# An attention block whose order of work is planned in Python: reciprocals of 16 columns, a broadcast in four transfers, and an order drawn from a table of seeds

## The chip, the core and the metric

The kernel runs on one core of a Trainium2 chip. Five engines matter here: TensorE (PE), VectorE (DVE), ScalarE (ACT), GpSimd (POOL) and SyncE (SP), which issues most of the transfers. Each engine takes its instructions in the order of the program and waits, at the head of its queue, for what the next one needs. The metric is the device time in microseconds (us) of the core. Three runs of the kernel before gave 408.4, 409.14 and 409.2; their median is 409.14 us.

## What is computed

The input is one sequence of 2048 tokens with 448 channels, 16 heads of 28 channels, everything in bf16:

```python
qkv = (x @ wqkv).reshape(B, S, 3, H, Dh)      # S = 2048, D = 448, H = 16, Dh = 28
scores = einsum("bhqd,bhkd->bhqk", q, k) * Dh ** -0.5
p = softmax(scores, axis=-1)
o = einsum("bhqk,bhkd->bhqd", p, v)
out = o.reshape(B, S, D) @ wo
```

Nothing is masked, so 16 x 2048 x 2048 scores need an exponential each.

## The kernel before, in words

**Tiles.** The heads are worked in four groups of four, the queries in four chunks of 512. A group and a chunk make a window; there are 16. In a window the keys come in 16 rows of 128, and a row has four tiles, one for each head: a tile is 128 keys by 512 queries. All in all there are 16 x 16 x 4 = 1024 tiles, each one score matmul (L917); two of them run side by side on two halves of PE's rows.

**Two ways to an exponential.** Pairs of tiles go into a two-bank PSUM tile `PA` (two of them), and ACT turns a pair into bf16 probabilities `PTA` in one instruction (L1337). The other tiles go singly into one of three banks `PD` and are turned into the bits of an exponential by a polynomial: `DU` (DVE, L1118), `DV` (DVE, L1121), `DG` (POOL, L1124) and `PTD` (DVE, L1137), or, for a few, one DVE copy to `SG` (L1050) and six POOL steps (L1057 to L1080). In the profile, 844 tiles go to ACT as 422 pairs, 155 go the way of DVE with one POOL step, and 25 the way of POOL.

**After the exponential.** PE multiplies the probabilities with the values `VA` and adds them up in the bank `PO` (L1182). One column in eight of `VA` is 1.0, so that some rows of `PO` hold the softmax's sums. When a window is through, `finish_window` runs a chain: DVE copies `PO` to `OSB` (L1002); SP sends the rows with the sums to `DCO`, spread over 128 partitions (L1009); DVE takes the reciprocals, `DRC` (L1011); SP sends them to a DRAM scratch `SCR` (L1012) and back, broadcast over the partitions, to `RRB` (L1014); POOL multiplies `OSB` by `RRB` into `OT` (L1017). The last window takes the reciprocals with DVE's block transposes instead (`norm_dve`, L929 to L933), and the output follows by matmuls with `WO` (L856, L876, L951, L1469).

**What sets the order.** No order is written out by hand. The kernel holds a list of operations (`Op`), each with an engine, a planned duration, a latency until others can use its result, what it depends on, and a priority. A loop at the end of the kernel plays them through in planned time: whenever an engine is free in the plan, it takes the ready operation with the lowest priority number (`try_static` for DVE, POOL and SP; `try_pe` and `try_act` for the other two). PE decides there whether the next tile goes to a free `PA` pair or to a free `PD` bank, that is, to ACT or to DVE, so the number of tiles on each way falls out of the planned times. What was planned is then written out, engine by engine, and the chip runs it in that order with real waits; planned times themselves are not in the program. Constants such as `P1`, `PTT`, `XLAT0`, `GLAT` and the numbers inside `Op(...)` are planned durations and latencies.

**The start.** SP loads one half of the first chunk of `x` and then `WQ`; ACT's queue loads `WK` and then the other half (L281, L286). PE transposes the chunk in two rounds of eight (L418) into four banks, ACT and DVE copy two of the four pieces each (L425), PE forms the first queries and keys (L534), ACT writes `QB` twice (L709, L711) and `KB` twice (L571), DVE reduces the keys to a bound (L562), and the exponentials begin.

Of the kernel before, what the change touches and what calls it, by code (L numbers as in the profile page):

```python
# [9 lines left out]
ACT = mybir.ActivationFunctionType  # L10
# [4 lines left out]
F32 = mybir.dt.float32  # L15
# [34 lines left out]
PTT = 1.12  # L50
PTS = 0.59
# [33 lines left out]
def kernel(  # L85
# [38 lines left out]
    GEND = 0  # L124
    GY = 0.5
# [17 lines left out]
    GLAT = 2.4  # L143
# [46 lines left out]
    XLAT0 = (4.0, 4.8)  # L190
# [49 lines left out]
    DCW = QW * NR // P  # L240
# [5 lines left out]
    SCR = [dram.tile([NR, QW], F32, name=f"SCR{i}") for i in range(2)]  # L246
# [164 lines left out]
    t0_bank = (PO[:], PA[1][:, 0:QW], PA[0][:, 0:QW], PA[0][:, QW:2 * QW])  # L411
# [9 lines left out]
    for cc in range(CC):  # L421
        eng = ("ACT", "DVE")[cc % 2]

        def ev0(cc=cc, eng=eng):
            (nc.scalar.copy if eng == "ACT" else nc.vector.tensor_copy)(  # L425
                out=XT[0][cc // 2][:, cc % 2, :], in_=t0_bank[cc].bitcast(BF16)[0:CK, 0:QW])
        xt0.append(add(Op(eng, 0.48 if eng == "ACT" else 0.36, ev0, deps=[t0[0][cc], t0[1][cc]], prio=-4999 + cc)))
# [53 lines left out]
    wkin = add(Op("SP", 0.01, None, prio=-1999, lat=5.1))  # L481
    wqin = add(Op("SP", 0.01, None, prio=-1998, lat=WQLAT))
    wvin = add(Op("SP", 0.01, None, prio=-1997, lat=11.0))
    for (W, WP, nm, win) in ((WK, WKP, "k", wkin), (WQ, WQP, "q", wqin)):
        w_ready[(nm, 0)] = add(Op("POOL", 1.0, pad_w(W, WP, 0), deps=[win], prio=-5001 + (nm == "k")))
# [181 lines left out]
    def task_Q(g, c):  # L667
# [38 lines left out]
        if w < NF:  # L706
            pq = -4390 if w == 0 else Q1P - 900
            if w == 0:
# [3 lines left out]
                    out=qb[1][:], in_=ap(), func=ACT.Identity, bias=offscol[:, 0:1], scale=YSC), deps=[ops[-1]], prio=pq + 15, lat=0.17))  # L712
# [17 lines left out]
            for i in range(HG):  # L730
                o = bound(i, [ab, kmaxop[0][0]] + ([e1] if w or i > 1 else []), pq + (20 if i < 2 else 40) + 0.01 * i)
# [261 lines left out]
    def finish_window(w, pvop):  # L993
# [11 lines left out]
        def rel(t):  # L1005
# [4 lines left out]
            out=DCO[b][:], in_=OSB[b][RS - 1::RS, :].rearrange("i (a b) -> i a b", b=DCW)), deps=[ev], prio=-10, lat=2.6))]  # L1010
        o2 = add(Op("DVE", 0.22, lambda: nc.vector.reciprocal(out=DRC[b][:], in_=DCO[b][:]), deps=o1, prio=-4000))  # L1011
        o3 = add(Op("SP", 0.4, lambda: nc.sync.dma_start(out=SCR[b][:].rearrange("i (a b) -> (i a) b", b=DCW),  # L1012
                                                         in_=DRC[b][:]), deps=[o2], prio=-10, lat=2.0))
        o4 = [add(Op("SP", 0.6, lambda: nc.sync.dma_start(  # L1014
            out=RRB[b][:], in_=bass.AP(SCR[b][:].tensor, SCR[b][:].offset, [[QW, NR], [0, RS], [1, QW]])),
            deps=[o3], prio=-10, lat=GLAT))]
# [205 lines left out]
    def try_pe(t):  # L1222
# [35 lines left out]
        if acts and not starved and (not TW or kmax_op[0].end is not None) and fits(MM, "S") and pos[0] < NT - NTAIL and s_ready(pos[0], t) and d_inflight[0] < ND + (OD > 0):  # L1258
# [4 lines left out]
            if free:  # L1263
# [37 lines left out]

    act_log = []
# [16 lines left out]
    def try_act(t):  # L1319
# [4 lines left out]
        if act_i[0] < len(acts):  # L1324
# [14 lines left out]
            op = Op("ACT", 0.0633 + 0.4267 * len(ns), fn, kind="E", lat=ELAT)  # L1339
# [18 lines left out]
    def try_static(e, t):  # L1358
        best = None
        for o in static[e]:  # L1360
            if o.elig is not None and not o.elig(t):
                continue
            if best is not None and o.prio >= best.prio:
                continue
            if o.kind == "sb" and (lock[0] > t + 1e-9 or YIELD and pool_waits(t)):
                continue
            if all(d.done(t) for d in o.deps) and (o.acq is None or o.acq(t)):
                best = o
# [13 lines left out]
    while True:  # L1382
# [12 lines left out]
        while progress:  # L1395
            progress = False
            for e in ("ACT", "PE", "POOL", "DVE", "SP"):
# [32 lines left out]
                seq += 1  # L1430
                heapq.heappush(ends, (o.end, seq, o))
# [74 lines left out]
```

## Time and profile before

One execution was profiled. Its own time was 408.98 us, 0.16 us under the median of the three runs; the span of its records is 407.2 us, so 1.8 us lie around the records.

| | busy, us | share of the span | instructions |
|---|---|---|---|
| PE | 358.5 | 88% | 2611 |
| DVE | 379.2 | 93% | 659 |
| ACT | 395.3 | 97% | 434 |
| POOL | 341.9 | 84% | 369 |

How to read it: a group's row gives line, engine, operation, output<-input, the count, the busy time of the group (overlaps counted once), the mean duration of one in ns, and the engine's idle time just before these instructions with what ended it. A record of ACT or DVE is longer than the distance to the next, because the next one begins before the last result is written. The clock of PE was granted in full in every slice of the span. The transfers move 17.16 MB, 42 GB/s on average.

### The profile page before, as it was taken

To read this page: it belongs to the slowest core of one execution; us is meant where nothing else is said; L and a number is where in the kernel's file an instruction comes from. 1 tells how busy PE (TensorE), PEld (TensorE's weight loads), DVE (VectorE), ACT (ScalarE), POOL (GpSimd) and SP (SyncE) were. 2 spreads that over 40 slices of the span, in tenths; PEclk is the share of its full clock that TensorE was granted. 3 is DMA by queue.
4 is the path that set the end of the run, shared out by engine and by line. 5 is a ranking of instruction groups with operands and counts; after the bars stand their busy time and mean duration, and the time that the engine had idled before them with its cause. 6 is when DMAs were issued, how large, how long until landed. Compare 5 with 4: busy or idle time off the path is not lost.

```text
span 407.2 us, 7611 instructions
## 1 busy us (share of the span) xinstructions
PE 358.5 (88%) x2611; PEld 119.8 (29%) x2621; DVE 379.2 (93%) x659; ACT 395.3 (97%) x434; POOL 341.9 (84%) x369
## 2 busy tenths in 40 slices
PE   8999988898888989889898988889799898889996
PEld 4343232322222232322323222232322222222222
DVE  5898899999999999999999999999999999999983
ACT  4999999999999999999999999999999999999994
POOL 4368988798698979999899898999678999989970
PEclk9999999999999999999999999999999999999999
DMA  9343030211501020110501001000230101010122
GB/s 222 42 71 84 6 71 9 36 27 26 119 10 31 20 44 19 20 35 15 106 21 32 23 15 34 11 29 21 72 60 6 37 13 31 1 52 2 50 74 90
DMA packets 36502, 17.16 MB, mean 42 GB/s; under 512 B 28721, under 2 KB 33329, under 8 KB 36465
## 3 DMA queue, kind: packets, MB, share of 16 engines
q1 hardware_dynamic: 35712, 16.25, 17.4%
q10 hardware_dynamic: 752, 0.44, 0.4%
q8 instruction: 20, 0.33, 0.3%
q14 instruction: 18, 0.14, 0.1%
HBM read 6.91 MB, written 2.33 MB: 23 GB/s over the span
## 4 chain that ended last, share of the span: by engine, by line
ACT 43%; DVE 22%; PE 11%; POOL 10%; issue 7%; DMA 4%; SPq 1%; ACTq 0%; DVEq 0%; POOLq 0%
ACT PTA L1337 43%; DVE PTD L1137 6%; DVE DU L1118 5%; POOL DG L1124 5%; DVE DV L1121 5%; PE PA L917 4%; PE PO L1182 3%; DMA RRB<-SCR 2%; PE PD L917 1%; POOL SG L1067 1%; POOL GV L1063 1%; SPq L464 1%; DMA XS<-in_x_dram 1%; DVE SG L1050 1%; DMA RRB<-RR 1%
## 5 line engine op out<-in xcount | busy, mean ns | idle before, releaser
L1337 ACT ACTIVATE PTA<-PA 128x1024 bf16<-128x1024 f32 x422 | 388.2, 1162 | 0.7 <-PE PA L917 0.6
L917 PE MATMUL PA<-QB,KB 64*128 64x512 bf16 x844 | 170.2, 380 | 33.9 <-ACT PTA L1337 30.9
L1124 POOL TENSOR_TENSOR DG<-DV,DU 128x512 f16<-128x512 f16 x155 | 177.2, 1155 | 21.1 <-DVE DV L1121 11.3
L917 PEld LDWEIGHTS <-KB 64*128 64x128 bf16 x1024 | 64.8, 93 | 173.1 <-issue 164.4
L1137 DVE SCALAR_TENSOR_TENSOR PTD<-PD,DG 128x512 uint16<-128x512 f32 x155 | 104.8, 682 | 7.6 <-POOL DG L1124 6.7
L1118 DVE TENSOR_SCALAR DU<-PD 128x512 f16<-128x512 uint16 x155 | 102.9, 680 | 3.6 <-PE PD L917 3.2
L1121 DVE SCALAR_TENSOR_TENSOR DV<-PD,DU 128x512 f16<-128x512 uint16 x155 | 103.7, 681 | 0.9
L1182 PE MATMUL PO<-PTA,VA 128*32 128x512 bf16 x844 | 85.5, 386 | 1.0 <-DVE QB L705 0.6
L917 PE MATMUL PD<-QB,KB 64*128 64x512 bf16 x180 | 66.0, 377 | 5.2 <-DVE PTD L1137 3.2
L1182 PE MATMUL PO<-PTD,VA 128*32 128x512 bf16 x180 | 54.8, 386 | 0.0
L1182 PEld LDWEIGHTS <-VA 128*32 128x32 bf16 x1024 | 19.6, 94 | 52.1 <-issue 51.3
L1063 POOL TENSOR_TENSOR GV<-GE,GU 128x512 f16<-128x512 f32 x25 | 28.9, 1156 | 2.7 <-DVE QP L740 1.7
L1067 POOL TENSOR_TENSOR SG<-SG,GU 128x512 f32<-128x512 f32 x25 | 28.9, 1155 | 1.8 <-DVE QP L740 1.0
L1065 POOL TENSOR_TENSOR GU<-GV,GU 128x512 f16<-128x512 f16 x25 | 28.8, 1154 | 1.2 <-DVE DRC L1011 0.5
L1017 POOL TENSOR_TENSOR OT<-OSB,RRB 128x512 bf16<-128x512 f32 x15 | 19.0, 1268 | 4.0 <-DMA RRB<-SCR 2.2
L1057 POOL TENSOR_SCALAR GU<-SG 128x512 f16<-128x512 uint16 x25 | 15.4, 617 | 6.0 <-DVE SG L1050 3.8
L695 PE MATMUL PO<-XT,WQP 112*128 112x512 bf16 x56 | 19.3, 386 | 0.6 <-DVE OSB L999 0.4
L1050 DVE COPY SG<-PD 128x512 f32<-128x512 f32 x25 | 17.0, 680 | 1.9 <-PE PD L917 1.9
L557 PE MATMUL PO<-XT,WKP 112*128 112x512 bf16 x52 | 17.2, 384 | 0.7 <-DVE QB L705 0.3
L772 PEld LDWEIGHTS <-XT 112*128 112x128 bf16 x256 | 14.0, 97 | 13.0 <-issue 12.5
L1060 POOL TENSOR_SCALAR GE<-SG 128x512 f32<-128x512 uint16 x25 | 15.4, 617 | 2.3 <-DVE PTD L1137 0.4
L1080 POOL TENSOR_SCALAR PTD<-SG 128x512 uint16<-128x512 f32 x25 | 15.5, 620 | 1.7 <-DVE QP L740 0.3
(119 smaller groups left out, 203.5 us busy)
## 6 DMA issues: line engine op xcount, KB each, us to landing
RRB<-SCR SPq DMA_DIRECT2D x15, 256.0 KB, 3.4
QB<-QP SPq DMA_DIRECT2D x56, 32.0 KB, 1.8
KB<-NK SPq DMA_DIRECT2D x12, 128.0 KB, 3.0
XS<-in_x_dram SPq DMA_DIRECT2D x2, 448.0 KB, 6.1
QB<-QB SPq DMA_DIRECT2D x28, 32.0 KB, 1.8
out_dram<-XS SPq DMA_DIRECT2D x2, 448.0 KB, 2.5
KB<-KB SPq DMA_DIRECT2D x6, 128.0 KB, 2.3
RRB<-RR SPq DMA_DIRECT2D x2, 256.0 KB, 3.4
```

The source lines that it names most:

```text
L695: ops = chain_mm(CC, lambda cc: nc.tensor.matmul(out=ap(), lhsT=WQP[g][:, cc, :], rhs=XT[c][cc // 2][0:CK, cc % 2, :], start=(cc == 0), st ...
L917: nc.tensor.matmul(out=ap, lhsT=KB[g % 2][i // 2][a:a + 64, j * P:(j + 1) * P], rhs=QB[w % NQB][i // 2][a:a + 64, :], start=True, stop=Tru ...
L1050: cp = add(Op("DVE", CPY, lambda: nc.vector.tensor_copy(out=X[:], in_=PX[slot.idx][:]), deps=[sop], prio=n - O1))
L1063: g3 = add(Op("POOL", PTT, lambda: nc.gpsimd.tensor_tensor(out=GV[:], in0=GE[:], in1=GU[:], op=ALU.mult), deps=[g2], prio=prio + 2, kind=" ...
L1065: g4 = add(Op("POOL", PTT, lambda: nc.gpsimd.tensor_tensor(out=GU[:], in0=GV[:], in1=GU[:], op=ALU.mult), deps=[g3], prio=prio + 3, kind=" ...
L1067: g5 = add(Op("POOL", PST, lambda: nc.gpsimd.tensor_tensor(out=X[:], in0=X[:], in1=GU[:], op=ALU.add), deps=[g4], prio=prio + 4, kind="g", ...
L1118: p1 = add(Op("DVE", P1, lambda: nc.vector.tensor_scalar(out=DU[b][:], in0=lo, scalar1=SIG / 65536, scalar2=SIG * (SS - 0.5), op0=ALU.mult ...
L1121: p2 = add(Op("DVE", P1, lambda: nc.vector.scalar_tensor_tensor(out=DV[b][:], in0=lo, scalar=65536 * (SS - 0.5 + CE / C3), in1=DU[b][:], o ...
L1124: gq = add(Op("POOL", PTT, lambda: nc.gpsimd.tensor_tensor(out=DG[b][:], in0=DV[b][:], in1=DU[b][:], op=ALU.mult), deps=[p2], prio=n, kind ...
L1137: f = add(Op("DVE", P1, lambda: nc.vector.scalar_tensor_tensor(out=PTD[st["s"].idx][:].bitcast(U16), in0=PX[slot.idx][:], scalar=EBITS + C ...
L1182: nc.tensor.matmul(out=PO[HP * st:HP * (st + 1), :], lhsT=VA[g][:, j, st, :], rhs=r["p"][i][1](), start=first, stop=last, tile_position=(0 ...
L1337: nc.scalar.activation(out=PTA[pslot.idx][:, 0:len(ns) * QW], in_=PA[s.idx][:, 0:len(ns) * QW], func=ACT.Exp, bias=ACT_BIAS, scale=ACT_SCALE)
```

## The change

It has five parts, all in the function of the kernel.

1. *Reciprocals of 16 columns.* `DCO`, `DRC` and the scratch shrink to a quarter: SP fetches only the last row of each 32 (4 rows instead of 16, since the rows of one head hold the same sum), so that DVE's reciprocal works on 128x16 numbers instead of 128x64.
2. *Broadcast by four transfers.* In place of one transfer that fills the 128 partitions of `RRB` there are four of 32 partitions each.
3. *Seeds.* A table of 44 numbers, one for each planned 10 us, feeds a hash. It moves the priorities of DVE's operations by up to 500 either way (`JPR`), the planned duration of a DVE operation by up to 0.01 us (`JIT`), and now and then keeps PE from giving a tile to a `PD` bank at that moment (`JSK`).
4. *Planned numbers.* `RCP` 0.19 in place of 0.22, latencies of the chain, `GLAT` 3.2 for 2.4, an exponential's 0.4261 for 0.4267, the loads at the start.
5. *The start.* `WK` is loaded behind the half of `x` on ACT's queue, the four transpose banks and the copying engines change places, and ACT's second write of `QB` comes behind the first write of `KB`. The later bounds of the queries wait for the first two.

Cut to its core:

```diff
+    SEEDS = (
+        17298, 16629, 52619, 43870, 52279, 2154, 27003, 43924, 59518, 53066, 23184, 45845, 40038, 43270, 58765, 51338,
...
+    )
+    SLICE = 10.0
+    JIT = 0.02
+    JPR = 1000
+    JSK = 0.02
...
-    XLAT0 = (4.0, 4.8)
+    XLAT0 = (3.9, 4.5)
...
-    DCW = QW * NR // P
+    DCW = QW * HG // P
...
-    nc.scalar.dma_start(out=WK[:, :, 0:GW], in_=wq3[:, :, D:D + GW])
     for b in range(NQC):
         if b == 0:
             for h, q in ((0, nc.sync), (1, nc.scalar)):
                 ts = slice(h * TPC // 2, (h + 1) * TPC // 2)
                 q.dma_start(out=XS[0][:, ts, :], in_=x_perm[:, ts, :])
+            nc.scalar.dma_start(out=WK[:, :, 0:GW], in_=wq3[:, :, D:D + GW])
...
-    t0_bank = (PO[:], PA[1][:, 0:QW], PA[0][:, 0:QW], PA[0][:, QW:2 * QW])
+    t0_bank = (PA[0][:, 0:QW], PO[:], PA[0][:, QW:2 * QW], PA[1][:, 0:QW])
...
-        eng = ("ACT", "DVE")[cc % 2]
+        eng = ("DVE", "ACT")[cc % 2]
...
         o1 = [add(Op("SP", 0.6, lambda: nc.sync.dma_start(
-            out=DCO[b][:], in_=OSB[b][RS - 1::RS, :].rearrange("i (a b) -> i a b", b=DCW)), deps=[ev], prio=-10, lat=2.6))]
-        o2 = add(Op("DVE", 0.22, lambda: nc.vector.reciprocal(out=DRC[b][:], in_=DCO[b][:]), deps=o1, prio=-4000))
+            out=DCO[b][:], in_=OSB[b][HP - 1::HP, :].rearrange("i (a b) -> i a b", b=DCW)), deps=[ev], prio=-10, lat=1.9))]
+        o2 = add(Op("DVE", RCP, lambda: nc.vector.reciprocal(out=DRC[b][:], in_=DCO[b][:]), deps=o1, prio=-4000))
         o3 = add(Op("SP", 0.4, lambda: nc.sync.dma_start(out=SCR[b][:].rearrange("i (a b) -> (i a) b", b=DCW),
-                                                         in_=DRC[b][:]), deps=[o2], prio=-10, lat=2.0))
-        o4 = [add(Op("SP", 0.6, lambda: nc.sync.dma_start(
-            out=RRB[b][:], in_=bass.AP(SCR[b][:].tensor, SCR[b][:].offset, [[QW, NR], [0, RS], [1, QW]])),
-            deps=[o3], prio=-10, lat=GLAT))]
+                                                         in_=DRC[b][:]), deps=[o2], prio=-10, lat=SLT))
+        o4 = [add(Op("SP", 0.6, lambda i=i: nc.sync.dma_start(
+            out=RRB[b][HP * i:HP * (i + 1), :], in_=SCR[b][i:i + 1, :].to_broadcast([HP, QW])),
+            deps=[o3], prio=-10 + 0.1 * i, lat=2.0)) for i in range(HG)]
...
-            if free:
+            if free and (JSK == 0.0 or draw(t, 31 * seq_now[0] + 7) >= JSK - 0.5):
...
+    def draw(t, n):
+        k = int(t / SLICE)
+        if k >= len(SEEDS) or SEEDS[k] == 0:
+            return 0.0
+        x = (SEEDS[k] * 2654435761 + n * 2246822519) & 0xFFFFFFFF
+        x = ((x ^ (x >> 15)) * 3266489917) & 0xFFFFFFFF
+        return (x ^ (x >> 13)) % 1000 / 1000 - 0.5
...
+            key = o.prio + (JPR * draw(t, id_of(o)) if e == "DVE" else 0.0)
+            if best is not None and key >= low:
                 continue
...
+                if e == "DVE":
+                    o.dur += JIT * draw(t, seq)
```

The written-out programs differ in these counts (before, after): pairs of tiles on ACT 422, 420; tiles by DVE and one POOL step 155, 159; tiles by POOL 25, 25; transfers issued by SP 213, 258. In the changed kernel's lines, L1009 to L1017 become L1020 to L1028, L1118 to L1137 become L1129 to L1148, and L1337 becomes L1362.

More of the change, by code (lines that the diff above doesn't have):

```diff
@@ L50 @@
 PTT = 1.12
+RCP = 0.19
 PTS = 0.59
@@ L245 @@
     FW = sb([P, 2 * NF, HP], BF16, "FW")
-    SCR = [dram.tile([NR, QW], F32, name=f"SCR{i}") for i in range(2)]
+    SCR = [dram.tile([HG, QW], F32, name=f"SCR{i}") for i in range(2)]
     OUTS = XS
@@ L484 @@
     for (W, WP, nm, win) in ((WK, WKP, "k", wkin), (WQ, WQP, "q", wqin)):
[L485 removed]
+        w_ready[(nm, 0)] = add(Op("POOL", 0.55, pad_w(W, WP, 0), deps=[win], prio=-5001 + (nm == "k")))
     for g in range(1, G):
@@ L711, in task_Q @@
                 e1 = add(Op("ACT", 0.62, lambda: nc.scalar.activation(
-                    out=qb[1][:], in_=ap(), func=ACT.Identity, bias=offscol[:, 0:1], scale=YSC), deps=[ops[-1]], prio=pq + 15, lat=0.17))
+                    out=qb[1][:], in_=ap(), func=ACT.Identity, bias=offscol[:, 0:1], scale=YSC), deps=[ops[-1], kev[(0, 0, 0)]], prio=pq + 15, lat=0.17))
                 quse.extend([e1])
```

18 lines of the change are left out of this document (12 added, 6 removed), and 2 rows, old and new, of the table SEEDS.

## The prediction

> **What bounds the kernel now.** I read the page's busy shares first, then its chain, then the groups of instructions, then the waits.
>
> ```profile
> span 407.2 us, 7611 instructions
> PE 358.5 (88%) x2611; PEld 119.8 (29%) x2621; DVE 379.2 (93%) x659; ACT 395.3 (97%) x434; POOL 341.9 (84%) x369
> ...
> ACT 43%; DVE 22%; PE 11%; POOL 10%; issue 7%; DMA 4%; SPq 1%; ACTq 0%; DVEq 0%; POOLq 0%
> ...
> L1337 ACT ACTIVATE PTA<-PA 128x1024 bf16<-128x1024 f32 x422 | 388.2, 1162 | 0.7 <-PE PA L917 0.6
> ```
>
> The chain changes engine all the time: the engines are near balance, with ACT ahead. The last row says what ends the time: 422 exponentials keep ACT busy for 388.2 us and leave it idle for 0.7. A record lasts 1162 ns, but records overlap; one pair costs the stream 388.2 / 422 = 0.92 us. That is the price to use.
>
> ```profile
> 10.69:399.58 388.89, 345.77 (x2510) 113.43 (x2519) 369.82 (x629) 388.30 (x423) 336.48 (x343) 1.00 0.16 37
> 40.00:390.00 350.00, 308.79 (x2215) 99.63 (x2224) 338.41 (x573) 349.40 (x381) 313.19 (x312) 1.00 0.14 33
> ```
>
> These are stretches; the columns are length, PE, PEld, DVE, ACT, POOL, granted clock, DMA share, GB/s. In the stream, from the first exponential (10.69) to the end of the last (399.58), ACT is busy 388.30 of 388.89 us. Between 40 and 390 us DVE is idle 350 - 338.4 = 11.6 us and POOL 36.8. So the time is a head of 10.7 us, a stream whose length is the number of pairs, and a tail of 7.6 us within the span.
>
> **The change part by part: pairs.** The reordered program has 420 pairs on ACT instead of 422; their four tiles go to DVE and POOL. On ACT that is -2 x 0.92 = -1.84 us. This holds in full only where nothing else keeps ACT waiting, so DVE has to have room.
>
> ```profile
> L1011 DVE RECIPROCAL DRC<-DCO 128x64 f32<-128x64 f32 x15 | 8.1, 542 | 0.0
> L930 DVE RECIPROCAL DR<-SG 128x16 f32<-128x16 f32 x1 | 0.3, 253 | 0.0
> ...
> 381.68 0.60 DVE DV L1121
> 382.28 0.60 DVE PTD L1137
> ...
> 385.25 0.54 DVE L1011 RECIPROCAL DRC<-DCO 128x64 f32<-128x64 f32 x1
> 385.70 0.56 DVE L863 CAST XS<-PD 128x448 bf16<-128x448 f32 x1
> ```
>
> A tile costs DVE three steps of 0.60 us (two rows of the chain's steps), so four tiles cost 12 x 0.60 = 7.2. A reciprocal of 64 columns takes 0.54 by its record and 0.45 to the next start (385.25 to 385.70); the tail's own reciprocal of 16 columns takes 0.25, which with the same overlap of 0.09 is 0.16. Fifteen of them save 15 x 0.29 = 4.3 us. DVE carries 7.2 - 4.3 = +2.9 us, against 11.6 idle: it fits on average. I also cut both written-out orders at the evictions of `PO` and weighed each stretch with such steps: in the old order DVE's work is up to 1.02 of ACT's in a stretch, in the new one at most 0.99, an estimate from counts and rows. POOL carries 4 x 1.12 (the chain's step of a `DG`, in the row below) = +4.5 of 36.8. PE multiplies the same 1024 tiles.
>
> ```profile
> 389.88 1.12 POOL DG L1124
> ```
>
> The seeds themselves cost the chip nothing: they only choose which ready operation DVE takes first, and whether a tile goes to a `PD` bank. What they can cost is a wait, where DVE takes up something less urgent and PE, which works in order, stands before a `PD` bank that is still in use, with the next pair for ACT queued behind it. One thing speaks for an order that holds on the chip: the old plan reckons 0.22 for a reciprocal whose step is 0.45, so that DVE falls 0.23 behind its plan in each window and makes that up in its idle time; the new plan reckons 0.19 for a step of about 0.16. And even with that error ACT loses next to nothing today.
>
> **The broadcast in four.** Per window, SP issues three transfers more, and `OT` on POOL waits for four. Behind them in SP's queue stand the moves to `QB` for a later window; these are 1.65 us later at most, and PE needs them a window on.
>
> ```profile
> RRB<-SCR SPq DMA_DIRECT2D x15, 256.0 KB, 3.4
> KB<-NK SPq DMA_DIRECT2D x12, 128.0 KB, 3.0
> KB<-NK SPq DMA_DIRECT2D x4, 64.0 KB, 2.4
> ...
> L1014 SPq DMA_DIRECT2D RRB<-SCR x15: 538/552/585, 58.3 to 387.5; - x15
> ```
>
> The columns of the first rows end in KB each and us from issue to landing; the last row has an issue's length, 552 ns. The fourth quarter is issued 3 x 0.55 = 1.65 us after the first. The nearest row for one quarter, a broadcast of 64 KB to 32 partitions, lands in 2.4 us: 1.65 + 2.4 = 4.05, so 0.65 us later than today's 3.4. Bounds: 1.8 us for a quarter (the same rows carried on down to no bytes: 2.4 - 0.6), so 3.45, no change; or 3.4, as long as today's whole, so 5.05, 1.65 later. I take 2.4. The smaller `DCO` and `SCR` may give back a few tenths. What a late `RRB` does can be read from the one place where it does harm today:
>
> ```profile
> 53.74 4.48 SPq L464 DMA_DIRECT2D WO<-in_wo_dram  x7
> 58.32 0.54 SPq L1014 DMA_DIRECT2D RRB<-SCR  x1
> ...
> 62.06 1.27 POOL L1017 TENSOR_TENSOR OT<-OSB,RRB 128x512 bf16<-128x512 f32 x1 [1.47 <-DMA RRB<-SCR]
> 66.71 0.69 DVE L1137 SCALAR_TENSOR_TENSOR PTD<-PD,DG 128x512 uint16<-128x512 f32 x1 [0.73 <-POOL DG L1124]
> 67.46 0.37 PE L917 MATMUL PD<-QB,KB 64*128 64x512 bf16 x1 [0.56 <-DVE PTD L1137]
> 68.58 1.02 ACT L1337 ACTIVATE PTA<-PA 128x1024 bf16<-128x1024 f32 x1 [0.40 <-PE PA L917]
> 69.78 10.32 ACT L1337 ACTIVATE PTA<-PA 128x1024 bf16<-128x1024 f32 x11 [0.17 <-PE PA L917]
> ```
>
> Seven loads of `WO` stand in SP's queue ahead of the broadcast; `RRB` is late, POOL waits 1.47 us, behind it DVE 0.73, PE 0.56, and ACT loses 0.40 + 0.17, all that it loses in the stream. So a wait of 1.47 on POOL costs ACT about 0.4 at once: some 1.07 are cushioned. A shift of 0.65 stays inside the cushion: 0. In the new order these loads stand ahead of `SCR` and only four loads of `WKP` ahead of the broadcast, so this stall should shrink: between 0 and -0.57, I take -0.3.
>
> [...]
>
> **The start.**
>
> ```profile
> 3.96 0.90 PEld L418 LDWEIGHTS <-XS 128*112 128x112 bf16 x8 [0.89 <-DMA XS<-in_x_dram]
> 5.17 0.57 PEld L418 LDWEIGHTS <-XS 128*112 128x112 bf16 x8 [0.31 <-DMA XS<-in_x_dram]
> 5.58 0.59 ACT L425 COPY XT<-PO 112x512 bf16<-112x512 bf16 x1 [2.56 <-PE PO L418]
> 5.69 0.42 DVE L425 COPY XT<-PA 112x512 bf16<-112x512 bf16 x1
> 7.95 0.69 ACT L709 ACTIVATE QB<-PD,offscol 128x512 bf16<-128x512 f32 x1 [1.30 <-PE PD L534]
> 8.17 0.69 DVE L562 TENSOR_REDUCE KPART<-PD 128x1 f32<-128x512 f32 x1 [1.06 <-PE PD L534]
> ...
> 3.00:4.00 1.00, 1.00 (x4) 0.11 (x2) 0.83 (x3) 0.02 (x1) 0.74 (x6) 1.00 1.18 316
> ```
>
> The second half of `x` leaves ACT's queue first now; PE waits 0.31 for it, so up to -0.31, and the first copy goes by DVE (0.42) instead of ACT (0.59): -0.17. Against it: the transfers already fill their engines (share 1.18, 316 GB/s), so the first half shares them with 224 KB instead of `WK`'s 98: 126 KB / 316 GB/s = +0.4 at worst. ACT's new order makes `KB` wait for the reduction (ends 8.86) with one write done instead of two: about +0.1. Range -0.4 to +0.5; I take -0.1.
>
> **The tail.**
>
> ```profile
> 392.27 5.75 SPq L870 DMA_DIRECT2D out_dram<-XS  x2
> ...
> 401.68 0.33 SPq L878 DMA_DIRECT2D out_dram<-XS  x1
> ...
> 403.23 1.37 SPq L1478 DMA_DIRECT2D out_dram<-XT  x3
> ...
> 404.00:405.00 1.00, 0.00 (x0) 0.00 (x0) 0.25 (x1) 0.34 (x1) 0.00 (x0) 1.00 0.68 230
> ```
>
> The second store of L870 (336 KB) is issued by 398 us today, ahead of the late tile's (L878, at 401.68). The new order puts it behind that one, at about 402, so that it still moves when the final stores start at 403.23. Those leave the DMA engines a third free (share 0.68, 230 GB/s): 336 KB at 230 GB/s would be 1.5 us, most of it gone by 404. Bounds 0 and +0.4; I take +0.2. DVE and POOL end before the last exponential, as now, so the four added tiles don't show there.
>
> **Sum.** -1.84 (pairs) - 0.3 (stall) - 0.1 (start) + 0.2 (tail) + 0.2 (my allowance for new waits of ACT in a denser DVE, bounded by 0 and by the whole 2.9 us) = -1.84, on the profiled execution's 408.98 us: 407.14. That execution is 0.16 below the median of 409.14, on which the same step gives 407.3.
>
> **Rivals.**
>
> *Quarters pay the full price (slower).* If a quarter lands as late as the whole did, 3.4 us, `RRB` is 1.65 later and 1.65 - 1.07 = 0.58 passes to ACT in each of 15 windows: +8.7, to 409.14 - 1.84 + 8.7 = 416.0. It decides from 2.82 us per quarter on; at 2.94 the gain is gone, at 3.0 the kernel is slower by over 0.2%. The rows of 64 and 128 KB speak against it, and the new order may have been given more distance there. 0.09, most of it near 410 to 412.
>
> [...] 0.04. [...]
>
> *DVE sets the pace (no change).* If the idle 11.6 us can't be used, because they lie where DVE waits for POOL, the +2.9 shows on ACT by way of PE. Two thirds of it, 1.9, undo the gain: 409.2. For it: DVE is at 97% in the stretch; against it: ACT's 0.6 idle at that load, and no stretch over 0.99. 0.1.
>
> *All of it (faster still).* Start -0.4, stall -0.57, no tail, no new waits: 409.14 - 1.84 - 0.97 = 406.3. For it: each term is inside its bounds, from rows. Against: all at once. 0.2.
>
> **How the numbers follow.** About 0.2% (0.8 us) is what a measurement of this kernel can tell from no change. The forecast case has 0.57, between 406.7 and 408.3. Faster: 0.57 + 0.2 = 0.77. Same: 0.14. Slower: 0.09. The range 406.0 to 408.9 holds the forecast, the third rival and, of the cases without change, the nearer half.
>
> **What would show it.** The exponentials' group: x420, about 386.4 us busy, idle under 1.5. Reciprocals at 0.25 by record. `OT` waits for `RRB` under 1.1 us at a time. First exponential between 10.3 and 11.2. Wrong if ACT's idle time in the stream exceeds 2 us: then the releaser behind PE's waits names the rival, POOL's `OT` or DVE's `PTD`.

## The result, and the profile after

The changed kernel took 407.94 us, the median of 12 runs (405.68 to 408.18), against 408.77 for the kernel before (12 runs, 408.4 to 410.42). The ratio is 0.9964, with a 95% interval of 0.9949 to 0.9978: faster by about 0.4%, and more than the 0.2% that can be told from no change. The twelve times fall into two groups, three between 405.68 and 405.89 and nine between 407.45 and 408.18, so that the median is one of the later group. The forecast of 407.3 us and its sign hold. But the start came out 1.9 us worse than forecast and the stream of exponentials 1.3 us better, each more than the 0.83 us by which the medians differ.

The profiled execution took 407.57 us, 1.41 less than that of before. The page of the changed kernel: span, busy shares, chain, the group of exponentials.

```profile
span 405.8 us, 7718 instructions
...
PE 359.6 (89%) x2622; PEld 122.5 (30%) x2622; DVE 382.8 (94%) x671; ACT 392.6 (97%) x432; POOL 346.8 (85%) x373
...
ACT 84%; PE 7%; issue 6%; DMA 1%; DVE 1%; ACTq 0%
...
L1362 ACT ACTIVATE PTA<-PA 128x1024 bf16<-128x1024 f32 x420 | 385.5, 1257 | 0.0
```

The chain lies on ACT for 84% of the span, where it was 43%, and DVE's share of it went from 22% to 1%. There are 420 pairs, and ACT is idle for 0.0 us before them. The stretches of the changed kernel (length, PE, PEld, DVE, ACT, POOL, granted clock, DMA share, GB/s):

```profile
12.48:398.12 385.64, 346.52 (x2528) 115.90 (x2525) 373.27 (x640) 385.64 (x422) 342.62 (x348) 1.00 0.15 34
40.00:390.00 350.00, 311.88 (x2248) 102.93 (x2247) 342.61 (x587) 350.00 (x383) 318.08 (x316) 1.00 0.14 32
```

So the span divides like this:

| | before, us | after, us | difference |
|---|---|---|---|
| head, to the first exponential | 10.69 | 12.48 | +1.79 |
| stream of exponentials | 388.89 | 385.64 | -3.25 |
| tail, to the end of the span | 7.6 | 7.7 | 0.0 |

The stream gained 1.4 us more than the two pairs are worth, and the head gave 1.79 back. Where the head lost them stands in the timeline (start, length, engine, line, operation, count, and in brackets the idle time before it with its releaser). First two rows of the kernel before, then the changed kernel.

```profile
6.21 0.40 PE L534 MATMUL PD<-XT,WQ 112*28 112x512 bf16 x4 [0.34 <-ACT XT L425]
6.43 0.40 PE L534 MATMUL PD<-XT,WK 112*28 112x512 bf16 x4
```

```profile
4.80 0.46 PE L429 MATMUL PA<-ident,XS 128*112 128x128 bf16 x2 [0.83 <-DMA XS<-in_x_dram]
...
7.06 0.62 PE L545 MATMUL PD<-XT,WK 112*28 112x512 bf16 x4 [0.30 <-DVE XT L436]
...
7.44 1.09 PE L545 MATMUL PD<-XT,WQ 112*28 112x512 bf16 x8
...
8.29 0.57 PE L545 MATMUL PD<-XT,WK 112*28 112x512 bf16 x4
...
8.69 0.39 PE L545 MATMUL PD<-XT,WQ 112*28 112x512 bf16 x4
...
8.91 0.39 PE L545 MATMUL PD<-XT,WK 112*28 112x512 bf16 x4
...
9.57 0.69 ACT L720 ACTIVATE QB<-PD,offscol 128x512 bf16<-128x512 f32 x1 [2.13 <-PE PD L545]
...
10.57 1.44 ACT L582 ACTIVATE KB<-PD,bndcol,selcol 128x512 bf16<-128x512 f32 x2 [0.31 <-DVE KPART L573]
...
12.48 1.94 ACT L1362 ACTIVATE PTA<-PA 128x1024 bf16<-128x1024 f32 x2
```

Three losses add up. The transposes start at 4.80 instead of 3.96 (+0.84): SP's half of `x` now lands after 4.0 us instead of 3.2, and PE stands idle for 0.83. Then the matmuls for the first queries and keys go at half their rate: between 7.06 and 8.69 lie four distances of about 0.41 us from one group of four to the next (the row of eight holds two groups), and from there on they are 0.22 (8.69, 8.91), where they were 0.22 from the first in the kernel before (6.21, 6.43). From the first group to `QB` it takes 2.51 us instead of 1.74 (+0.77). Last, `KB` waits 0.31 for DVE's reduction, and from `QB` to the first exponential it takes 2.91 instead of 2.74 (+0.17). The column of the granted clock reads 1.00 in these first microseconds of both kernels and doesn't show the half rate; the distances of the matmuls do. The trace's list of clock changes agrees with the distances: its first entry of the full clock is at 5.31 us before and at 8.65 after.

### The profile page after: what moved, and what is told of

Read it like the earlier page. It is cut to its first block, busy times and chain, and to the rows that moved or that the text cites. A ratio compares the mean times of both kernels' runs of the same rounds, so it can differ in the third digit from the quotient of the medians.

```text
span 405.8 us, 7718 instructions
## 1 busy us (share of the span) xinstructions
PE 359.6 (89%) x2622; PEld 122.5 (30%) x2622; DVE 382.8 (94%) x671; ACT 392.6 (97%) x432; POOL 346.8 (85%) x373
## 4 chain that ended last, share of the span: by engine, by line
ACT 84%; PE 7%; issue 6%; DMA 1%; DVE 1%; ACTq 0%
ACT PTA L1362 84%; PE PA L928 2%; PE PO L1193 2%; DMA XS<-in_x_dram 1%; PE PD L867 1%; PE PD L545 1%; ACT KB L582 0%; PE PD L928 0%; PE PA L429 0%; PE PO L783 0%; PE PO L867 0%; PE PD L962 0%; ACT RR L989 0%; PE PD L1499 0%; DVE SG L940 0%
## 5 line engine op out<-in xcount | busy, mean ns | idle before, releaser
L1362 ACT ACTIVATE PTA<-PA 128x1024 bf16<-128x1024 f32 x420 | 385.5, 1257 | 0.0
L928 PE MATMUL PA<-QB,KB 64*128 64x512 bf16 x840 | 165.3, 380 | 39.5 <-ACT PTA L1362 36.3
L1135 POOL TENSOR_TENSOR DG<-DV,DU 128x512 f16<-128x512 f16 x159 | 182.5, 1154 | 18.4 <-DVE DV L1132 12.5
L928 PEld LDWEIGHTS <-KB 64*128 64x128 bf16 x1024 | 68.9, 93 | 176.8 <-issue 167.5
L1129 DVE TENSOR_SCALAR DU<-PD 128x512 f16<-128x512 uint16 x159 | 106.7, 682 | 4.6 <-PE PD L928 3.9
L1148 DVE SCALAR_TENSOR_TENSOR PTD<-PD,DG 128x512 uint16<-128x512 f32 x159 | 107.2, 681 | 1.2 <-POOL DG L1135 0.4
L1132 DVE SCALAR_TENSOR_TENSOR DV<-PD,DU 128x512 f16<-128x512 uint16 x159 | 107.3, 682 | 1.1
L1028 POOL TENSOR_TENSOR OT<-OSB,RRB 128x512 bf16<-128x512 f32 x15 | 19.1, 1270 | 0.4 <-DVE PTD L1148 0.4
```

Of the source, the lines that this page charges most:

```text
L928: nc.tensor.matmul(out=ap, lhsT=KB[g % 2][i // 2][a:a + 64, j * P:(j + 1) * P], rhs=QB[w % NQB][i // 2][a:a + 64, :], start=True, stop=Tru ...
L1028: o5 = add(Op("POOL", 1.22, lambda: nc.gpsimd.tensor_tensor(out=OT[g][c][:], in0=OSB[b][:], in1=RRB[b][:], op=ALU.mult), deps=o4, prio=-10 ...
L1129: p1 = add(Op("DVE", P1, lambda: nc.vector.tensor_scalar(out=DU[b][:], in0=lo, scalar1=SIG / 65536, scalar2=SIG * (SS - 0.5), op0=ALU.mult ...
L1132: p2 = add(Op("DVE", P1, lambda: nc.vector.scalar_tensor_tensor(out=DV[b][:], in0=lo, scalar=65536 * (SS - 0.5 + CE / C3), in1=DU[b][:], o ...
L1135: gq = add(Op("POOL", PTT, lambda: nc.gpsimd.tensor_tensor(out=DG[b][:], in0=DV[b][:], in1=DU[b][:], op=ALU.mult), deps=[p2], prio=n, kind ...
L1148: f = add(Op("DVE", P1, lambda: nc.vector.scalar_tensor_tensor(out=PTD[st["s"].idx][:].bitcast(U16), in0=PX[slot.idx][:], scalar=EBITS + C ...
```

## The experiments

In all of them the order of each engine is that of the changed kernel unless the text says otherwise. Four were timed side by side: the changed kernel again, its start in two variants, and the new loads alone in the kernel before (beside them the kernel before itself took 408.66 us, median of 17). A ratio is always to the kernel before, with its 95% interval in brackets.

### The changed kernel again

> The changed kernel once more, for another profile: its times came in groups at 405.7 and at 408.2. Theory A: the profile shows which group it belongs to by its start alone; the stretch from the first exponential to the end of the last lasts 385.5 to 385.8 us in either group, and the tail after it 7.6 to 7.8. Rival B: the groups differ in the tail by 2 us. Rival D (a stall of ACT in the stream that comes in some runs): the stretch differs.

It took 407.55 us (9 runs), ratio 0.9965 [0.9946, 0.9984]. Its times fall into two groups, four between 405.66 and 406.32 and five between 407.55 and 408.54. The profiled run is of the later group, with the first exponential at 12.45 us and the same stream, 385.64. No run of the earlier group was profiled here; two variants further down, with the same start, came early by chance (10.60 and 10.67 us).

### The old order of the loads

```diff
+    nc.scalar.dma_start(out=WK[:, :, 0:GW], in_=wq3[:, :, D:D + GW])
     for b in range(NQC):
...
-            nc.scalar.dma_start(out=WK[:, :, 0:GW], in_=wq3[:, :, D:D + GW])
```

> The changed kernel with the loads at the start in their old order (WK first on ACT's queue, then the half of x); every engine's order is otherwise the same. Theory A (the start): the first half of x lands near 3.9 us again, the transposes follow the warm-up matmuls without a gap, the key and query matmuls of L545 follow each other at 0.21 us a group from the first on, and the first exponential comes at 10.6 to 10.9 us instead of 12.48. The time falls by 1.8 to 2.5 us against the changed kernel's median, to 405.4 to 406.2, and the runs no longer spread over 2.5 us. Rival B (the lost time sits in the tail, where the 336 KB store stands behind the late tile's): no change, 407.5 to 408.2 with the same spread. Rival C (ACT's new order of QB and KB costs it): the first exponential stays above 11.5.

It took 406.01 us (6 runs), ratio 0.9949 [0.9932, 0.9966]; four runs lie between 405.78 and 406.11 and two at 407.86. From its timeline:

```profile
3.77 0.40 PE L429 MATMUL PA<-ident,XS 128*112 128x128 bf16 x2
...
5.09 0.32 PE L429 MATMUL PA<-ident,XS 128*112 128x128 bf16 x2 [0.59 <-DMA XS<-in_x_dram]
...
6.15 0.40 PE L545 MATMUL PD<-XT,WK 112*28 112x512 bf16 x4 [0.41 <-DVE XT L436]
6.36 0.61 PE L545 MATMUL PD<-XT,WQ 112*28 112x512 bf16 x8
...
10.80 2.86 ACT L1362 ACTIVATE PTA<-PA 128x1024 bf16<-128x1024 f32 x3
```

No gap of PE ahead of the transposes, full rate from the first group, and the first exponential 1.68 us earlier, with the stream the same to 0.01 us (385.63). In these two profiles, moving that one load costs the changed kernel 1.7 us of its head. Between the medians it is 1.5 us, less than the 1.8 to 2.5 expected, and the runs still spread over 2.1 us. The wait of 0.59 us for the other half, ahead of 5.09, comes when the clock is full already (from 3.96), and doesn't bring it down: the groups behind it still follow at 0.21 us (6.15, 6.36). The two runs at 407.86 were not profiled; that they started late again is likely, but not shown.

### The new loads in the kernel before

The same line is moved the other way, behind the half of `x`, in the kernel before.

> The kernel before with only the loads in the new order (the half of x first on ACT's queue, WK behind it). Theory A: it gets what the change got at its start, the first exponential at 12.0 to 13.0 instead of 10.69, and is slower by 1.3 to 2.5 us: 410.1 to 411.3. Rival B or C: no change, 408.4 to 409.2.

It took 409.82 us (9 runs, 407.93 to 410.78), ratio 1.002 [1.0004, 1.0036]: slower, but by less than expected. These runs, too, fall into two groups, four between 407.93 and 408.62 and five between 409.82 and 410.78; the profiled one is of the later group.

```profile
4.71 0.46 PE L418 MATMUL PO<-ident,XS 128*112 128x128 bf16 x2 [0.74 <-POOL bndcol L330]
...
11.93 1.94 ACT L1337 ACTIVATE PTA<-PA 128x1024 bf16<-128x1024 f32 x2
```

The move alone makes the old kernel's first exponential 1.24 us later, by the same gap (0.74 us here; POOL's tile is only what the row names last).

### Two more warm-up matmuls

Is the late `x` itself the loss, or PE's idle time while it waits? Here the loads stay new and `x` late, but PE gets two more of the matmuls on zeros that it runs at the start, so that it doesn't stand still.

```diff
-        nc.tensor.matmul(out=warm_bank, lhsT=zeros[:], rhs=zrow[:], start=True, stop=True)
+        warm_open[0] += 1; [nc.tensor.matmul(out=warm_bank, lhsT=zeros[:], rhs=zrow[:], start=True, stop=True) for _ in range(3 if warm_open[0] == NWARM else 1)]
```

> The changed kernel, loads as changed, with two more warm-up matmuls on zeros at the start of PE (six in place of four; about 0.95 us more). Theory A, its second half (the gap on PE before the transposes costs the full clock for one more stretch): the key and query matmuls go at 0.21 us a group from the first on although x lands at about 4.8 us; the first exponential comes at 11.2 to 11.7, and the time is 406.2 to 407.0. If only the landing of x counts and the gap does not: the groups stay at 0.4 us until 8.6 us and the time stays at 407.5 to 408.2. Rival B: no change.

It took 406.36 us (5 runs, 405.69 to 406.55), ratio 0.994 [0.9928, 0.9952].

```profile
2.06 2.76 PE L417 MATMUL PA<-zrow,zeros 128*128 128x512 bf16 x6
...
6.62 0.40 PE L545 MATMUL PD<-XT,WK 112*28 112x512 bf16 x4 [0.40 <-DVE XT L436]
6.84 0.61 PE L545 MATMUL PD<-XT,WQ 112*28 112x512 bf16 x8
...
11.27 2.86 ACT L1362 ACTIVATE PTA<-PA 128x1024 bf16<-128x1024 f32 x3
```

`x` is late as before (transposes at 4.62), and yet the first exponential comes 1.2 us earlier than in the changed kernel, and no run lies in the later group. So it is PE's idle time, and not the late data, that goes with the late full clock (from 5.75 us here, from 8.65 in the changed kernel); what is left of the late start, 11.27 - 10.69 = 0.6 us, is the late data itself (the transposes start 0.66 us later than before) and the new order on ACT.

The other runs add to this by chance, since `x` doesn't land at the same time in each execution (with the new loads its first half landed between 3.5 and 4.0 us after its issue). All the profiles, by PE's gap ahead of the transposes (no gap and the new warm-up first; the kernels not told of yet come below):

| kernel | gap, us | full clock from, us | first exponential, us |
|---|---|---|---|
| before | none | 5.31 | 10.69 |
| old loads | none | 3.96 | 10.80 |
| old loads, both `QB` first | none | 4.31 | 10.61 |
| two more warm-ups | none | 5.75 | 11.27 |
| two more warm-ups, both `QB` first | none | 6.81 | 11.48 |
| reciprocals of 64 columns | 0.27 | 3.95 | 10.60 |
| eight broadcasts | 0.41 | 4.67 | 10.67 |
| one broadcast | 0.62 | 8.50 | 12.29 |
| no seeds, timed | 0.71 | 8.69 | 12.44 |
| before, new loads | 0.74 | 8.27 | 11.93 |
| changed again | 0.80 | 8.63 | 12.45 |
| no seeds, first run | 0.82 | 9.95 | 13.12 |
| changed | 0.83 | 8.65 | 12.48 |

Up to 0.41 us of gap the full clock comes between 3.95 and 6.81 us; from 0.62 on, between 8.27 and 9.95. The length of the gap doesn't give the moment: without any gap it lies anywhere between 3.96 and 6.81. And with reciprocals of 64 columns the full clock comes at 3.95, just ahead of the gap's start at 3.98, so that this run doesn't show what a gap of 0.27 us does; the one of 0.41, from 3.98 to 4.39, does lie ahead of its full clock at 4.67. What sets the moment isn't settled here, and no run has a gap between 0.41 and 0.62.

### Reciprocals of 64 columns again

The changed kernel's order, with the reciprocals, `DCO` and the scratch at their old size:

```diff
-    DCW = QW * HG // P
+    DCW = QW * NR // P
...
-    SCR = [dram.tile([HG, QW], F32, name=f"SCR{i}") for i in range(2)]
+    SCR = [dram.tile([NR, QW], F32, name=f"SCR{i}") for i in range(2)]
...
-            out=RRB[b][HP * i:HP * (i + 1), :], in_=SCR[b][i:i + 1, :].to_broadcast([HP, QW])),
+            out=RRB[b][HP * i:HP * (i + 1), :], in_=SCR[b][4 * i + 3:4 * i + 4, :].to_broadcast([HP, QW])),
```

> The changed kernel, order of all engines kept, with reciprocals of 64 columns again (DCO, DRC and the scratch at their old size; the four transfers read one row of each four). It is judged by its stream, from the first exponential to the end of the last (385.6 us in the changed kernel), since the start varies by 2 us from run to run. DVE carries 15 x 0.29 = 4.3 us more, against about 7.4 us that it is idle between 40 and 390. Theory E (DVE has room for both): ACT's idle time in the stream stays under 0.5 us, stream 385.6 to 386.2. Theory F (the smaller reciprocal is what makes the four moved tiles fit): ACT loses 1 to 4 us, stream 386.6 to 389.6, by way of PE waiting for DVE's PTD.

A single run: 405.75 us, first exponential at 10.60, stream 385.71. The rows for the reciprocal and the exponentials, and the middle stretch:

```profile
L1022 DVE RECIPROCAL DRC<-DCO 128x64 f32<-128x64 f32 x15 | 8.2, 544 | 0.0
...
L1362 ACT ACTIVATE PTA<-PA 128x1024 bf16<-128x1024 f32 x420 | 385.6, 1254 | 0.0
```

```profile
40.00:390.00 350.00, 313.85 (x2251) 102.65 (x2251) 344.94 (x587) 350.00 (x383) 318.00 (x316) 1.00 0.15 34
```

DVE does 2.3 us more in the middle stretch (344.94 against 342.61), where 4.3 was expected, and keeps 5.1 idle; ACT loses 0.07 us. Once the order is fixed, the smaller reciprocal is worth nothing measurable. It can still have helped the planner to find that order; this wasn't tried.

### One broadcast, and eight

The broadcast back in one transfer of 128 partitions, from the small scratch:

```diff
-        o4 = [add(Op("SP", 0.6, lambda i=i: nc.sync.dma_start(
-            out=RRB[b][HP * i:HP * (i + 1), :], in_=SCR[b][i:i + 1, :].to_broadcast([HP, QW])),
+        o4 = [add(Op("SP", 0.6, lambda i=i: None if i else nc.sync.dma_start(
+            out=RRB[b][:], in_=bass.AP(SCR[b][:].tensor, SCR[b][:].offset, [[QW, HG], [0, HP], [1, QW]])),
```

> The changed kernel, order kept, with the broadcast in one transfer of 128 partitions again. Theory G (the split costs and brings nothing on the path): stream 385.6 to 385.8, OT waits for RRB 0 to 0.5 us in all; RRB is issued in one go and lands about 3.2 us later, against the fourth quarter's issue plus 2.1 us, so it is there up to half a us earlier or later. Rival H (four transfers bring RRB sooner, and that is part of the gain): OT waits over 1 us in all and the stream grows by 0.3 to 1 us.

A single run: 407.8 us, stream 386.31, 0.67 more than with four. First the changed kernel's rows for the broadcast: the group `OT` and the issues with their landing from its page, then the issues' lengths at their line (min, median, max in ns).

```profile
L1028 POOL TENSOR_TENSOR OT<-OSB,RRB 128x512 bf16<-128x512 f32 x15 | 19.1, 1270 | 0.4 <-DVE PTD L1148 0.4
...
RRB<-SCR SPq DMA_DIRECT2D x60, 64.0 KB, 2.1
```

```profile
L1025 SPq DMA_DIRECT2D RRB<-SCR x60: 302/419/1700, 61.3 to 388.0; - x60
```

And the run with one transfer, its group `OT` and, from its timeline, the longest of the waits:

```profile
L1028 POOL TENSOR_TENSOR OT<-OSB,RRB 128x512 bf16<-128x512 f32 x15 | 19.0, 1269 | 5.3 <-DMA RRB<-SCR 4.6 <-DVE PTD L1148 0.3
```

```profile
100.30 0.59 SPq L1025 DMA_DIRECT2D RRB<-SCR  x1
...
106.27 1.26 POOL L1028 TENSOR_TENSOR OT<-OSB,RRB 128x512 bf16<-128x512 f32 x1 [2.49 <-DMA RRB<-SCR]
```

With four transfers `OT` is idle for 0.4 us in all, and no row names `RRB`; with one it waits 4.6 us for `RRB` in four windows (0.31, 2.49, 0.41 and 1.42), and the stream grows as rival H said. In those windows the one transfer is there 5.0 to 6.0 us after its issue begins (here 100.30 to 106.27), far later than the 3.4 of the kernel before, which read 16 rows of the scratch, each for eight partitions, instead of four for 32 each. The trace shows a difference between the two: both have 128 packets of 2 KB, but these start within 1.3 us in the kernel before (issue at 100.92) and over 3.8 us here, and their landing is told by sixteen updates of the semaphore there (2.76 to 3.46 us after the issue) and here by four (5.53 to 5.83) behind one at 1.01. What makes the difference isn't shown.

The four quarters take about 1.5 + 2.1 = 3.6 us (the fourth is issued some 1.5 after the first, and one lands in 2.1), 0.2 more than the one transfer before. So with the small scratch the split saves time, and against the old scratch it costs next to none.

In the other direction, eight transfers of 16 partitions:

```diff
-        o4 = [add(Op("SP", 0.6, lambda i=i: nc.sync.dma_start(
-            out=RRB[b][HP * i:HP * (i + 1), :], in_=SCR[b][i:i + 1, :].to_broadcast([HP, QW])),
+        o4 = [add(Op("SP", 0.6, lambda i=i: [nc.sync.dma_start(
+            out=RRB[b][HP * i + k:HP * i + k + 16, :], in_=SCR[b][i:i + 1, :].to_broadcast([16, QW])) for k in (0, 16)],
```

> The changed kernel, order kept, with the broadcast in eight transfers of 16 partitions: four issues more, so RRB is there about 4 x 0.42 = 1.7 us later. In the changed kernel RRB is there between 0.2 and 5 us ahead of OT. Theory of the prediction (a late RRB is cushioned for some 1.07 us before ACT sees it): POOL's OT waits for RRB in 5 to 10 windows, 3 to 8 us in all, ACT loses 0 to 2 us, stream 385.6 to 387.6. Rival (each wait of POOL passes on to ACT in full): stream 388.6 or more.

A single run: 407.45 us, with an early start (10.67) and a stream of 387.63, 1.99 more than with four and 0.03 beyond the range of the prediction's theory. The group `OT`, and the row of the issues:

```profile
L1028 POOL TENSOR_TENSOR OT<-OSB,RRB 128x512 bf16<-128x512 f32 x15 | 19.0, 1269 | 7.3 <-DVE DU L1129 2.8 <-DMA RRB<-SCR 2.4 <-DVE DV L1132 1.0
```

```profile
RRB<-SCR SPq DMA_DIRECT2D x120, 32.0 KB, 1.8
```

The last piece is there some 7 x 0.42 + 1.8 = 4.7 us after the first issue. The group's row puts 2.4 of 7.3 us down to `RRB` and 3.8 to DVE's `DU` and `DV`. But `OT` reads neither of them, and a wait for several things is put down to one of them by its end. From the timeline, one of these waits:

```profile
99.39 3.76 SPq L1025 DMA_DIRECT2D RRB<-SCR  x8
...
103.64 1.28 DVE L1129 TENSOR_SCALAR DU<-PD 128x512 f16<-128x512 uint16 x2
...
104.81 1.27 POOL L1028 TENSOR_TENSOR OT<-OSB,RRB 128x512 bf16<-128x512 f32 x1 [1.89 <-DVE DU L1129]
```

The eighth issue begins at 102.74, and its landing is told at 104.51, just ahead of `OT`; the second `DU` is still going on when `OT` starts. By the semaphores in the trace, the last piece of `RRB` ends `OT`'s wait in eight windows, 7.2 us in all. So the prediction's theory holds (5 to 10 windows, 3 to 8 us), and the rival by which each wait passes on in full (388.6 or more) falls. How a wait gets to ACT shows behind one of the two longest, in the same way as behind the loads of `WO` in the kernel before:

```profile
130.76 1.27 POOL L1028 TENSOR_TENSOR OT<-OSB,RRB 128x512 bf16<-128x512 f32 x1 [1.89 <-DMA RRB<-SCR]
...
133.19 0.69 DVE L1148 SCALAR_TENSOR_TENSOR PTD<-PD,DG 128x512 uint16<-128x512 f32 x1 [0.90 <-POOL DG L1135]
133.93 0.37 PE L928 MATMUL PD<-QB,KB 64*128 64x512 bf16 x1 [0.52 <-DVE PTD L1148]
...
136.16 1.02 ACT L1362 ACTIVATE PTA<-PA 128x1024 bf16<-128x1024 f32 x1 [0.53 <-PE PA L928]
```

SP is held twice as long with each broadcast (3.76 us for the eight issues above, about 4 x 0.42 = 1.7 for four), so the moves behind it in its queue are later too; what they cost isn't told apart.

### The order without the seeds

The three amplitudes at zero, so that the planner makes its order without the table:

```diff
-    JIT = 0.02
-    JPR = 1000
-    JSK = 0.02
+    JIT = 0.0
+    JPR = 0
+    JSK = 0.0
```

The plan then has 421 pairs and 158 tiles with one POOL step.

> The changed kernel with JIT, JPR and JSK at 0: no seeds, everything else of the change stays. The written-out order has 421 pairs on ACT (420 with the seeds, 422 before). Theory I (the seeds are worth one pair, the rest comes with the smaller reciprocal and the planned numbers): stream 385.6 + 0.92 = 386.5 to 386.9, ACT's idle time under 0.3. Rival J (the seeds also choose an order without stalls): ACT's idle time 0.5 us or more, stream 387.0 to 389.

A single run: 415.28 us, ACT idle for 4.9 in a stream of 391.88. Part of this came from a clock that was halved in the middle of the run (the stretch's columns as above, the clock third from the end):

```profile
124.00:128.00 4.00, 3.73 (x21) 1.54 (x20) 3.54 (x6) 3.43 (x4) 3.18 (x3) 0.50 0.00 0
```

Whether the order brings that about was the question for a second, timed, run.

> The changed kernel with the three amplitudes of the seeds at zero, as in the single look at 415.28 us, now timed in rounds. If the order alone is the cause: every run near 415, ACT again idle by some 5 us in the stream, and the granted clock again halved near 120 us. If that look was a chance event of the clock: most runs below 411 (421 pairs, 0.92 us more than the changed kernel, and at most 2 us of waits), and the profile's granted clock at 1.00 throughout the stream.

It took 411.63 us (4 runs, 411.5 to 412.73), ratio 1.0068 [1.005, 1.0085]: slower than the kernel before. The clock of the profiled run stayed at 1.00, so its fall was not the order's regular effect; but "most below 411" failed too. The stream is 388.84 us, 3.20 longer than with the seeds, in the range of rival J: one pair (0.92) and one wait of ACT (2.56), together 0.3 more than the difference. Its timeline, SP's rows first:

```profile
105.91 2.04 SPq L664 DMA_DIRECT2D KB<-NK  x3
108.06 1.22 SPq L760 DMA_DIRECT2D QB<-QB  x2
109.37 1.17 SPq L766 DMA_DIRECT2D QB<-QP  x2
110.59 1.43 SPq L664 DMA_DIRECT2D KB<-NK  x1
...
114.08 0.61 PE L928 MATMUL PA<-QB,KB 64*128 64x512 bf16 x4 [0.32 <-DMA KB<-NK]
...
114.57 2.85 ACT L1362 ACTIVATE PTA<-PA 128x1024 bf16<-128x1024 f32 x3 [2.56 <-PE PA L928]
```

The last of four moves that complete the next group's keys stands in SP's queue behind four moves to `QB`. PE's first score of that group waits for it, and ACT loses 2.56 us; the first run has the same wait at the same place (2.43 at 115.12). With the seeds all four moves go at 104.27, one behind the other:

```profile
104.27 2.74 SPq L664 DMA_DIRECT2D KB<-NK  x4
```

So this table of seeds is worth 409.8 - 405.8 = 4.0 us of span between two profiled runs that both started late, 3.2 in the stream and 0.8 in the tail (by the ratios 1.0068 and 0.9965, 1.0%), and the rest of the change without it would have lost 0.7%. Most of that is one move in one queue; what other seeds would give wasn't tried.

### A better start

ACT's second write of `QB` goes back in front of the writes of `KB`, with the old loads:

```diff
-                e0 = add(Op("ACT", 0.62, lambda: nc.scalar.activation(
-                    out=qb[0][:], in_=ap(), func=ACT.Identity, bias=offscol[:, 0:1], scale=YSC), deps=[ops[-1]], prio=pq, lat=0.17))
-                e1 = add(Op("ACT", 0.62, lambda: nc.scalar.activation(
-                    out=qb[1][:], in_=ap(), func=ACT.Identity, bias=offscol[:, 0:1], scale=YSC), deps=[ops[-1], kev[(0, 0, 0)]], prio=pq + 15, lat=0.17))
+                e0 = add(Op("ACT", 0.62, lambda: [nc.scalar.activation(
+                    out=qb[k][:], in_=ap(), func=ACT.Identity, bias=offscol[:, 0:1], scale=YSC) for k in range(2)], deps=[ops[-1]], prio=pq, lat=0.17))
+                e1 = add(Op("ACT", 0.62, lambda: None,
+                    deps=[ops[-1], kev[(0, 0, 0)]], prio=pq + 15, lat=0.17))
```

> The changed kernel with WK loaded ahead of the half of x, and ACT's second write of QB back in front of the writes of KB. Theory (the start's clock and the order on ACT are separate terms): full clock from about 4.0 us, first exponential at 10.6 (0.17 before that of the old loads alone, 10.80), stream 385.6, median 405.8 to 406.0. Rival (the second write in front delays KB, as the plan of the changed kernel says): KB starts at 9.1 or later instead of 8.89, first exponential at 11.0 or later, median 406.2 or more.

It took 405.74 us (5 runs, 405.62 to 406.02), ratio 0.9918 [0.9904, 0.9933], the fastest of all.

```profile
9.03 1.45 ACT L582 ACTIVATE KB<-PD,bndcol,selcol 128x512 bf16<-128x512 f32 x2
...
10.61 3.77 ACT L1362 ACTIVATE PTA<-PA 128x1024 bf16<-128x1024 f32 x4
```

`KB` starts 0.14 us later than with the old loads alone (8.89), the way the rival said though not as far (9.1), but the first exponential comes 0.19 earlier: ACT has no second write left to do in between. The same with the new loads and the two more warm-up matmuls:

> The changed kernel with its own loads, two more warm-up matmuls, and ACT's second write of QB in front of the writes of KB. Theory: no gap on PE, full clock from about 5.7 us, first exponential at 11.1 (0.17 before that of the two matmuls alone, 11.27), stream 385.6, median 406.0 to 406.3 and no run above 407. Rival (the gap is not what makes some runs slow): some of the runs at 407.5 or more.

It took 406.14 us (5 runs, 405.52 to 406.59), ratio 0.9927 [0.9913, 0.9942]; no run lies in the later group. The profiled execution's first exponential came at 11.48 instead of 11.1, since its full clock began at 6.81 us (the table above) instead of 5.7.

## Why the prediction was right, and by what errors

The sum, term by term, on the profiled executions:

| term | forecast, us | measured, us |
|---|---|---|
| pairs | -1.84 | -1.84 |
| stall behind the loads of `WO` | -0.3 | -0.6 |
| waits of ACT in the stream | +0.2 | -0.8 |
| start | -0.1 | +1.79 |
| tail | +0.2 | 0.0 |
| sum | -1.84 | -1.45 (own times: -1.41) |

**Pairs: right.** 420 pairs at 385.5 / 420 = 0.918 us. The bound was ACT and still is. DVE took the added tiles: it is busy 4.2 us more in the middle stretch (342.61 against 338.41; forecast +2.9) and keeps 7.4 idle. The reciprocal's record is 243 ns (forecast 0.25), but what the fifteen gave back was mis-sized: 2.3 us by the run with 64 columns, not 4.3. The rival by which DVE sets the pace fell here, and once more where DVE had 2.3 us of reciprocals to add.

**Stall: right in sign, its size read too small.** ACT's idle time in the stream went from 388.89 - 388.30 = 0.59 to 0.00, and no row has `OT` wait for `RRB`. But `RRB` is not there sooner: it lands at 64.8 us instead of 61.9, and the new order has `OT` start only at 66.00. And the idle time isn't the whole stall, as the next term shows: the two starts behind it in the kernel before come 1460 and 1196 ns after the ones ahead of them, 0.85 us more than two distances of 904. By that measure the stall was beyond my bound of 0.57, and 0.3 us of the row for waits belong to it.

**New waits: wrong sign.** I allowed +0.2 and got -0.8, what the stream lost beyond the pairs and the stall (3.25 - 1.84 - 0.59). I had read ACT's idle 0.7 as all that waits cost before. But records of ACT overlap (before, they are 1162 ns long at a mean distance of 921.2), so that a short wait doesn't show as idle. The distances between the starts of exponentials show it: their mean went from 921.2 ns to 917.4, and those over 925 ns (other work of ACT in between included) went from 36 of 421 to 19 of 419. The new order removed short waits that the idle column hides. It also made new, very short ones, which the mean alone doesn't show: distances of at most 904 ns went from 286 to 100, and those between 905 and 924 from 99 to 300. Nearly all of these 300 are near 916 ns, and in 288 of them ACT starts less than 0.1 us after the semaphore that tells of PE's scores. So it looks as if ACT, idle for 0.0 us by its records, still waits some 12 ns for PE's scores in most pairs: 300 x 12 ns = 3.6 us, an estimate. Whether an order can get them back wasn't tried. That the seeds remove the long ones, and not another part, follows from the run without them only in part: its loss is one long wait.

**The broadcast: right, on the safe side.** I took 2.4 us for a quarter and an issue of 0.55; it is 2.1 and 0.42. The rival of the full price, which decides from 2.82 us a quarter on, fell with that 2.1. Behind the chance of 0.04 that stands in the 0.14 for no change is a time for a quarter that no run shows; the runs showed 2.1 us, and the fourth quarter there about 3.6 us after the first is issued, 0.2 later than the one transfer before. The cushion is there, but not as one number. With 1.07 us for each wait, the waits of 2.49 and 1.42 with one transfer would cost ACT 1.8 us, and the two of 1.89 with eight 1.6; the streams lost 0.67 and 1.99.

**Start: the step that failed.** "-0.1, range -0.4 to +0.5" measured +1.79. Two things in it were mis-sized. The first half of `x` lands 0.8 us later and not 0.4 "at worst": the share of 126 KB at 316 GB/s was too small a price for two halves in flight together. It varies, too: with the same loads it landed after 3.5 and 3.6 us in the two variants that started early, against 4.0 here and 3.2 before. And I counted only the delay of the data. The working nowhere asked what PE does in that time: it stands idle 0.83 us right behind its warm-up matmuls, and its full clock then begins at 8.65 instead of 5.31 us. That cost 0.77 on the way to `QB`, on top of the 0.84. My bound on the first exponential, 10.3 to 11.2, is broken by 1.3 us. `KB` waiting for the reduction was forecast at +0.1 and is +0.17.

**Tail: 0.0**, inside its bounds. The second store does go behind the late tile's, at 400.51 us, and costs nothing that shows.

So the interval held by luck, because the stream did 1.3 us better than forecast and the start 1.9 worse; and with most of the runs in the earlier group (405.7 to 406.3 us in the two measurements) the median would have been at the lower end of the stated range, 406.0, or below it. With the start as forecast the kernel would have come near the rival of "all of it", 406.3, which the old loads reach (406.01).

## What to carry to other kernels

Before a load at the start is moved, look at what PE does until the data come: here a gap of 0.62 to 0.83 us behind the warm-up went with a full clock from 8.3 us on or later, where runs without such a gap had it by 6.8, and two more matmuls on zeros closed it. On ACT here, whose records overlap, the idle column undercounts the waits (0.59 us in the stream before, where two starts behind one stall came 0.85 late); compare the distances between starts with their floor, the commonest distance included. An order found for planned times should be run with its critical transfers in view: here one move behind four others in a queue cost more than two pairs (2.56 us against 1.84).

## What the runs showed that was not expected

- The clock column of the profile reads 1.00 in a stretch in which matmuls go at half rate, before the trace's first entry of the clock (groups some 0.41 us apart until 8.69, 0.22 after).
- One broadcast of 256 KB from four rows of DRAM was there 5.0 to 6.0 us after its issue began, in the four windows where POOL waited for it; one from 16 rows landed after 3.4, and four quarters of it after about 3.6.
- A wait for several things can be put down to one that wasn't needed: with eight broadcasts the row names `RRB` for 2.4 us of `OT`'s waits, and by the semaphores it was 7.2.
- In the single run without the seeds the clock fell to 0.50 for 13.7 us from 119.2 us on, in a stretch (116 to 120) in which PE was busy for 2.74 of 4 us. It did not do so in the timed run's profile with the same order, where PE was busy for 2.93 us of that stretch, and what sets it off stays open.
